# Query features turned by transposing DMAs instead of TensorE, and a table of offsets on the scheduler's priorities

## The chip, the cores and the metric

The kernel runs on one core of a Trainium2 chip. The metric is the device time of one execution in microseconds (us); lower is better. The core's engines are called as the profile calls them: PE (TensorE matmuls) and PEld (its weight loads), DVE (VectorE), ACT (ScalarE), POOL (GpSimd) and SP (SyncE, which in this kernel issues every DMA). Each engine works through its own queue in order and waits on semaphores.

## The reference

Two attention layers over 2048 tokens, 1024 columns and 32 heads of 32 columns are computed from separate inputs, and their outputs stand side by side. All data are float32.

```python
# A: four segments of 512 tokens; softmax attention inside a segment, a linear memory between them
logits = einsum("bhqd,bhkd->bhqk", qs, ks) * scale + mask
a_dot  = einsum("bhqk,bhkd->bhqd", softmax(logits), vs)
a_mem  = einsum("bhld,bhde->bhle", phi(qs), M) / (einsum("bhld,bhd->bhl", phi(qs), z)[..., None] + 1e-6)
o = g * a_mem + (1.0 - g) * a_dot          # then o @ wo
# B: linear attention with learned features
pq, pk = q @ w_phi, k @ w_phi              # per head
phi_q = concat([softmax(pq), softmax(-pq)]);  phi_k = concat([softmax(pk), softmax(-pk)])
kv, z = einsum("bhsf,bhsd->bhfd", phi_k, v), einsum("bhsf->bhf", phi_k)
o = einsum("bhqf,bhfd->bhqd", phi_q, kv) / (einsum("bhqf,bhf->bhq", phi_q, z)[..., None] + 1e-6)   # then o @ wo
```

The change lies in B's query side: a head has 64 features (32 of each softmax), a token 2048 in all.

## The kernel before, in words

Float32 accuracy is had from float16 matmuls: every operand is split into a high half (a rounded copy, made on ACT) and a low half (the rest, made by a subtraction on DVE or POOL), and each product is three matmuls: high by high, high by low, low by high. Products with large weights are done in seven block products of 512 columns by Strassen's scheme (`strassen`, L572 for loads of its operand and L584 for its matmuls) or block by block (`product`, L370).

The program has these stages in time: A's projections and attention together with the preparation of B's weights and inputs (to about 870 us); B's values and key features, which end in `kls`, the key-value sums of 32 heads split into halves (to about 1260 us, L1445); B's query features and output (1240 to 1565 us); A's output projection (L1636, from 1565 us to the end). The stages overlap at their seams.

In the query stage the 2048 tokens are 16 chunks of 128. For every pair of chunks, `strassen` makes four results of 128 tokens by 512 columns. `expo` turns each into `e`, 128 tokens by 1024 float32 features, with maxima, minima, two subtractions (L1238 to L1242, DVE), four exponentials (ACT) and sums (L1248, DVE). For each chunk and each half `hb` of the heads (32 times in all) there follow:

- POOL multiplies `e` by the key sums (L1550) and DVE reduces to denominators `dn` (L1553 to L1561); POOL multiplies `e` by the result (L1563).
- PE turns `e` so that features lie on partitions: eight float32 transposes of 128 by 128 into PSUM (L1569), in two groups of four. ACT copies each group of four, scaled by 2**14, to float16 (L1571), and DVE makes the low half from the same PSUM bank (L1573). The two halves are `pt`.
- PE multiplies `pt` by `kls` in 24 small matmuls (L1582, tile `pv`), and ACT and DVE split the result into `ot` (L1586, L1588).

When both halves of a chunk's `ot` are there, `project` multiplies them by B's output weight: twice 24 matmuls of 128 by 512 into a `misc` bank (L370), a scaled copy by ACT (L1463) and a store issued by SP (L1465).

The order of all instructions on each engine is not the order of the code. `Graph.op` records every operation with an engine, an estimated duration, what it reads and writes, and a priority `prio`; `Graph.run` then walks a clock, and at each step, for the engine that can start first, emits the operation with the smallest priority among those that could start then. Priorities are numbers per unit of work: in the query stage a chunk c has `P = Q0 + c`, `strassen` has `P - 1.2`, the features `P` and `project` `P + 1.1`. Estimated durations, DMA transfer times included, so decide the order, and the hardware then follows that order with its own durations. Tiles come from pools with a fixed number of buffers: `e` has five, `pt` three, `ot` four.

## Time and profile before

| | us |
|---|---|
| median of 3 runs | 1734.23 (1733.72 to 1735.37) |
| the profiled execution's own time | 1733.96 |
| its span, first to last instruction | 1732.3 |
| PE busy in the span | 1697.2 |
| DVE busy | 1384.0 |
| ACT busy | 1157.8 |
| POOL busy | 939.5 |

Busy time is the time in which at least one instruction of an engine was in work. Matmuls overlap each other in the pipeline, so what a matmul costs is read from the distance between the starts of successive ones and not from its duration: in a run of 128 by 512 matmuls the starts are 0.216 us apart, where the duration of one is given as 0.38 us. The profile's idle times of an engine are put down to what ended them.

### The profile page before, as it was taken

The page shows a single profiled execution, that of the slowest core. Times are in us where ns is not written, and L with a number is a line of the kernel's source. Part 1 is how long each engine was busy: PE and PEld are TensorE (multiplying, and loading weights), DVE is VectorE, ACT ScalarE, POOL GpSimd, SP SyncE. Part 2 cuts the span into 40 slices and gives each one's busy share as a digit, 9 for nine tenths or more (in the row PEclk, how much of TensorE's full clock was granted, in tenths as well). Part 3 has the DMA queues.
Part 4 walks back from the last instruction along what each step waited for, and adds up shares of the span by engine and source line. Part 5 has one row for each costly group of instructions (what it writes and reads, how often), then busy time and mean ns, then how long its engine had stood idle before and what let it go on. Part 6 is the DMA issues. An engine that isn't in the chain of part 4 may idle for free.

```text
span 1732.3 us, 39104 instructions
## 1 busy us (share of the span) xinstructions
PE 1697.2 (98%) x14664; PEld 1030.3 (59%) x14664; DVE 1384.0 (80%) x3269; ACT 1157.8 (67%) x2131; POOL 939.5 (54%) x1184
## 2 busy tenths in 40 slices
PE   8999999999999999999999999999999999999999
PEld 6667666767776676776754444444545555554444
DVE  6889899999997787889874988877978877786541
ACT  8788889888888798677772676765545544444331
POOL 3346477754478866656651777645737675440000
PEclk9999999999999999999999999999999999999999
DMA  6556455775666664743467474567413332234311
GB/s 210 160 166 185 151 169 174 223 209 169 224 181 185 188 165 122 227 162 106 136 179 262 131 240 130 180 211 251 161 44 118 103 111 85 63 139 146 122 66 63
DMA packets 194141, 273.62 MB, mean 158 GB/s; under 512 B 72224, under 2 KB 125216, under 8 KB 187424
## 3 DMA queue, kind: packets, MB, share of 16 engines
q1 hardware_dynamic: 193952, 271.13, 49.5%
q8 instruction: 115, 1.88, 0.4%
q14 instruction: 74, 0.61, 0.1%
HBM read 160.12 MB, written 85.00 MB: 142 GB/s over the span
## 4 chain that ended last, share of the span: by engine, by line
PE 40%; DVE 11%; ACT 2%; POOL 1%; issue 1%; POOLq 0%; ACTq 0%; DVEq 0%
PE proj L584 14%; PE misc L370 7%; PE proj L1636 5%; PE s L1636 2%; PE proj L370 2%; PE s L584 2%; DVE mx L1238 2%; PE misc L1636 1%; DVE r L1248 1%; PE pv L1582 1%; PE misc L584 1%; PE s L1569 1%; DVE e L1240 1%; DVE dn L1553 1%; DVE e L1242 1%; DVE pt L1389 1%
## 5 line engine op out<-in xcount | busy, mean ns | idle before, releaser
L370 PE MATMUL proj<-S,S 128*128 128x128 f16 (+1 forms) x3072 | 507.1, 300 | 4.3 <-DVE S L405 1.9
L370 PEld LDWEIGHTS <-S 128*128 128x128 f16 x4608 | 328.7, 98 | 151.2 <-issue 10.8
L584 PE MATMUL proj<-S,S 128*128 128x512 f16 x1584 | 360.6, 379 | 2.4 <-ACT cs L590 2.4
L584 PEld LDWEIGHTS <-S 128*128 128x128 f16 x2016 | 192.7, 98 | 221.7 <-issue 3.3
L960 POOL TENSOR_SCALAR_AFFINE_SELECT ph<-ph 128x256 f16<-128x256 f16 (+1 forms) x448 | 191.6, 450 | 172.5 <-DVE ph L954 133.7
L852 DVE CUSTOM_DVE_ANT_0 s<-s,causal 128x512 f32<-128x512 f32 (+3 forms) x512 | 242.6, 510 | 10.3 <-PE s L846 7.0
L954 DVE SCALAR_TENSOR_TENSOR ph<-s,ph 128x512 f16<-128x512 f32 x320 | 209.6, 683 | 51.5 <-ACT ph L953 49.3
L953 ACT ACTIVATE ph<-s 128x512 f16<-128x512 f32 x320 | 190.2, 659 | 0.3
L370 PE MATMUL misc<-S,ot 128*128 128x512 f16 x768 | 174.9, 380 | 0.0
L1245 ACT ACTIVATE e<-e,sk 128x256 f32<-128x256 f32 x256 | 113.4, 498 | 65.5 <-DVE e L1242 60.8
L370 PEld LDWEIGHTS <-ot 128*128 128x128 f16 x768 | 73.4, 98 | 81.8 <-issue 0.9
L846 PE MATMUL s<-S 96*128 96x512 f16 (+3 forms) x512 | 113.9, 299 | 2.2 <-DVE ph L954 1.6
L947 PE MATMUL s<-S 104*128 104x512 f16 (+3 forms) x512 | 113.1, 299 | 2.2 <-DVE ph L954 1.5
L951 ACT ACTIVATE s<-s,os 128x512 f32<-128x512 f32 x160 | 106.2, 717 | 6.9 <-PE s L947 5.3
L1550 POOL TENSOR_TENSOR e<-e,zb 128x512 f32<-128x512 f32 x64 | 80.2, 1277 | 55.7 <-DVE r L1248 35.1
L951 ACT ACTIVATE s<-s,bd 128x512 f32<-128x512 f32 x160 | 105.4, 705 | 6.5 <-PE s L947 6.4
L370 PE MATMUL proj<-wv,S 128*128 128x128 f16 x1536 | 101.8, 219 | 0.0
L983 PEld LDWEIGHTS <-ph 128*128 128x128 f16 x2560 | 87.3, 96 | 18.1 <-issue 2.2
L983 PE MATMUL pv<-vl,ph 128*128 128x66 f16 (+1 forms) x2560 | 91.9, 184 | 2.0 <-DVE oall L987 1.0
L1248 DVE TENSOR_REDUCE r<-e 128x32 f32<-128x1024 f32 x64 | 77.1, 1206 | 16.2 <-ACT e L1245 16.2
L1563 POOL TENSOR_TENSOR e<-e,r 128x1024 f32<-128x1024 f32 x32 | 61.9, 1938 | 34.5 <-DVE r L1561 27.5
L852 DVE DVE_READ_ACCUMULATOR2_ANT mt<- 128x1 f32 x512 | 72.6, 142 | 0.0
(344 smaller groups left out, 3344.1 us busy)
## 6 DMA issues: line engine op xcount, KB each, us to landing
S<-xf_d SPq DMA_DIRECT2D x126, 256.0 KB
S<-h SPq DMA_DIRECT2D x192, 128.0 KB
S<-wf_d SPq DMA_DIRECT2D x21, 1024.0 KB
st<-bwqk SPq DMA_DIRECT2D x64, 256.0 KB
out<-os SPq DMA_DIRECT2D x40, 256.0 KB
S<-aw SPq DMA_DIRECT2D x16, 512.0 KB
wa_d<-S SPq DMA_DIRECT2D x16, 512.0 KB
wf_d<-fo SPq DMA_DIRECT2D x32, 256.0 KB
```

The source lines that it names most:

```text
L370: op(PE, dur, lambda c=c, a=a, b=b, lv=lv, rv=rv: nc.tensor.matmul(pv(), lv(), rv(), start=(c == 0 and a + b == 0), stop=(c == n - 1 and a ...
L584: op(PE, 0.215, lambda n=n, a=a, b=b, lv=lv, rv=rv: nc.tensor.matmul(ps(), lv(), rv(), start=(start and n == 0 and a + b == 0), stop=(n == ...
L846: nc.tensor.matmul(ps()[:, o:o + 128 * i + 128], st()[0:96, 0, h, 128 * i:128 * i + 128], st()[0:96, 1, h, 0:128 * i + 128], start=True, s ...
L852: dve(0.12 + 0.00113 * n, lambda h=h, i=i, o=o, n=n: nc.vector.tensor_tensor_reduce(ps()[:, o:o + n], ps()[:, o:o + n], causal[:, 512 - n: ...
L947: nc.tensor.matmul(ps()[:, o:o + n], st()[0:104, 1, h, 128 * j:128 * j + 128], st()[0:104, 0, h, 128 * j:512], start=True, stop=True)
L951: act(0.59, lambda: nc.scalar.activation(ps(), ps(), AF.Exp, bias=0.0, scale=bdv()[:, 3, i2, 0:1]), r=[(bd, i2)], w=[ps])
L953: act(0.5, lambda: nc.scalar.activation(ph()[:, 0], ps(), AF.Copy, scale=2.0 ** 14), r=[ps], w=[(ph, 0)])
L954: dve(0.6, lambda: nc.vector.scalar_tensor_tensor(ph()[:, 1], ps(), 2.0 ** 14, ph()[:, 0], op0=OP.mult, op1=OP.subtract), r=[ps, (ph, 0)], ...
L960: nc.gpsimd.affine_select(pd, pd, pattern=[[0, n], [1, 128]], compare_op=OP.is_ge, fill=0.0, base=0, channel_multiplier=-1)
L983: nc.tensor.matmul(ps()[:, i, n0:n1], ph()[:, a, o:o + 128], vl()[:, j, h, n0:n1], start=(i == 0 and a == 0), stop=(j == min(i, 2)), skip_ ...
L1245: op(ACT, 0.41, lambda i=i: nc.scalar.activation(e()[:, 4 * i:4 * i + 4], e()[:, 4 * i:4 * i + 4], AF.Exp, bias=0.0, scale=sk()[:, i:i + 1 ...
L1636: op(PE, 0.215, lambda n=n, a=a, b=b: nc.tensor.matmul(ps(), v(a)[:, n, :], wform[w]()[:, b, n, :], start=(start and n == 0 and a + b == 0 ...
```

## The change

The change has two parts.

First, the query features are turned by DMA. After POOL's last multiplication, ACT makes the float16 high half directly from `e` in SBUF (two instructions of 128 by 512), DVE subtracts it from `e` to get the low half (two instructions, now `tensor_tensor` between SBUF tiles), and both halves go into a new tile `eh`, which is taken from the same five buffers as `e`. One DMA then transposes all sixteen 128 by 128 float16 blocks of `eh` into `pt`, 512 KB per DMA. The eight PE transposes and the PSUM banks they used are gone. The factor 2**14, which ACT and DVE applied, is now folded into the small row `r` before POOL's multiplication. The planner is told 0.6 us of SP and about 4.2 us to landing for such a DMA.

Second, `Graph.op` numbers the stretches of consecutive recorded operations that have the same priority ("jobs") and adds an offset from the table `MOVES`, by engine and job, to the priority of each operation in it. The table has 238 entries, from -43 to +21.5, spread over jobs 20 to 363; jobs are recorded in the order of the code, from A's first unit to the last chunks of the query stage. Since priorities alone choose between operations that are ready, the table changes the order on all five queues through most of the program.

```diff
+MOVES = {
+    "PE": {
+        20: -6.5, 22: -12.5, 76: -7, 79: -15.5, 83: -4, 96: -5, 101: 2, 102: 4, 104: 2, 107: 5.5, 108: 15.5, 113: 1.5,
...
     def op(self, eng, dur, fn, r=(), w=(), prio=0, lat=0.0, short=False, port=False, need=(), kb=256):
+        if prio != self.job[0]:
+            self.job = prio, self.job[1] + 1
+        prio += MOVES.get(eng, {}).get(self.job[1], 0.0)
...
+    def ev(e):
+        return e().rearrange("p h s d -> p (h s d)")
+
...
-            op(DVE, 0.1, lambda d1=d1, r=r: nc.vector.tensor_tensor(
-                r(), r(), d1()[:, :, None].to_broadcast([128, 16, 2]), op=OP.mult), r=[d1, r], w=[r], prio=P)
+            op(DVE, 0.1, lambda d1=d1, r=r: nc.vector.scalar_tensor_tensor(
+                r(), r(), 2.0 ** 14, d1()[:, :, None].to_broadcast([128, 16, 2]), op0=OP.mult, op1=OP.mult), r=[d1, r], w=[r], prio=P)
...
             pt = G.buf("b", [128, 2, 8, 128], F16, "pt", 3)
+            eh = G.buf("b", [128, 16, 2, 32], F32, "e", 5)
+
+            def hv(eh=eh):
+                return eh().rearrange("p h s d -> p (h s d)").bitcast(F16).rearrange("p (a n) -> p a n", a=2)
+
             for q in range(2):
-                ps = bank("s", [128, 4, 128])
-                for i in range(4):
-                    op(PE, 0.11, lambda q=q, i=i, e=e, ps=ps: nc.tensor.transpose(
-                        ps()[:, i, :], pairs(e)[:, 4 * q + i, :], ident), r=[e], w=[ps], prio=P)
-                op(ACT, 0.55, lambda q=q, pt=pt, ps=ps: nc.scalar.activation(pt()[:, 0, 4 * q:4 * q + 4], ps(), AF.Copy, scale=2.0 ** 14),
-                   r=[ps], w=[(pt, (0, q))], prio=P)
-                op(DVE, 0.62, lambda q=q, pt=pt, ps=ps: nc.vector.scalar_tensor_tensor(
-                    pt()[:, 1, 4 * q:4 * q + 4], ps(), 2.0 ** 14, pt()[:, 0, 4 * q:4 * q + 4], op0=OP.mult, op1=OP.subtract),
-                   r=[ps, (pt, (0, q))], w=[(pt, (1, q))], prio=P)
+                op(ACT, 0.53, lambda q=q, e=e, hv=hv: nc.scalar.activation(
+                    hv()[:, 0, 512 * q:512 * q + 512], ev(e)[:, 512 * q:512 * q + 512], AF.Copy), r=[e], w=[(eh, (0, q))], prio=P)
+                op(DVE, 0.7, lambda q=q, e=e, hv=hv: nc.vector.tensor_tensor(
+                    hv()[:, 1, 512 * q:512 * q + 512], ev(e)[:, 512 * q:512 * q + 512], hv()[:, 0, 512 * q:512 * q + 512], op=OP.subtract),
+                   r=[e, (eh, (0, q))], w=[(eh, (1, q))], prio=P, port=True)
+            op(SP, 0.6, lambda pt=pt, hv=hv: nc.sync.dma_start_transpose(
+                pt().rearrange("p a g t -> p (a g) t"), hv().rearrange("p a n -> p (a n)")),
+               r=[(eh, (a, q)) for a in range(2) for q in range(2)], w=[pt], prio=P, lat=2.0, kb=512)
```

What the orders of instructions become is shown at three places, each before and after. Names are those of the tiles; line numbers of the kernel after are 26 to 33 higher than those of the kernel before for the same statement.

PE in the query stage, at the end of a `strassen` (tile `proj`). Before, twelve transposes of `e` into an `s` bank stand here, and then a chunk's `project` (tile `misc`, from `ot`):

```order
L584 LDWEIGHTS S_14955
L584 MATMUL proj<-S_19188,S_14955 128x512
L1569 MATMUL s<-ident,e 128x128 x12
L370 LDWEIGHTS ot
L370 MATMUL misc<-S_19610,ot 128x512
```

After, at the end of a `strassen` of the same stage:

```order
L610 LDWEIGHTS S_15057
L610 MATMUL proj<-S_19210,S_15057 128x512
L1615 LDWEIGHTS kls
L1615 MATMUL pv<-pt,kls 64x128
L1615 LDWEIGHTS kls
```

The transposes are gone, and the products of `pt` and `kls` follow directly; they now wait for a DMA.

SP in the query stage. Before, a chunk's stores of the output (`out<-os`) stand together, then the loads of the next operand of `strassen` (`xf_d`):

```order
L1511 DMA wo_d<-cs 256x1x512
L1480 DMA h_20449<-awo 128x1024
L1465 DMA out<-os 128x512 x3
L572 DMA S_13978<-xf_d 128x1024 x4
L572 DMA S_14955<-xf_d 128x1024
```

After, transposing DMAs and stores of the output take turns:

```order
L1494 DMA out<-os 128x512
L1606 DMA_TRANSPOSE pt<-e 128x16x128
L1494 DMA out<-os 128x512
L1606 DMA_TRANSPOSE pt<-e 128x16x128
L1494 DMA out<-os 128x512
L1540 DMA wo_d<-cs 256x1x512
```

A store in this queue waits until ACT has copied the `project` result, and a transposing DMA behind it waits as long.

DVE at the seam between the key features and the query stage, around the last subtraction that makes `kls` (of the half of the heads that comes second). Before:

```order
L1440 TENSOR_TENSOR ez<-ez,zs 128x512
L1240 TENSOR_TENSOR e<-cs,mx 128x16x32
L1242 TENSOR_TENSOR e<-mx,cs 128x16x32
L1238 TENSOR_REDUCE mx<-proj 128x16
L1573 SCALAR_TENSOR_TENSOR pt<-s,pt 128x512 x2
L1238 TENSOR_REDUCE mx<-proj 128x16
L1242 TENSOR_TENSOR e<-mx,proj 128x16x32
L1445 TENSOR_TENSOR kls<-ez,kls 128x512
L1573 SCALAR_TENSOR_TENSOR pt<-s,pt 128x512 x2
```

After:

```order
L620 TENSOR_TENSOR proj<-cs,proj 128x512
L1589 RECIPROCAL d_19679<-d_19679 128x16
L1585 TENSOR_TENSOR dn<-dn,r 128x32
L1264 TENSOR_REDUCE mx<-cs 128x16
L1590 SCALAR_TENSOR_TENSOR r<-r,d_19679 128x32
L1587 SCALAR_TENSOR_TENSOR d_19690<-dn 128x16
L1474 TENSOR_TENSOR kls<-ez,kls 128x512
L1603 TENSOR_TENSOR e<-e 128x512 x2
```

Before, this last row of `kls` stands behind six of the subtractions that split query features (L1573; two of the six are shown). After, it stands ahead of all of them (L1603).

More of the change, by code (lines that the diff above doesn't have):

```diff
@@ L56 @@
 EUP = 2.0 ** 15
+MOVES = {
[6 rows of a table added]
+    "DVE": {
[4 rows of a table added]
+    "ACT": {
[3 rows of a table added]
+    "POOL": {
+        59: 0.5, 67: 5.5, 70: -0.5, 93: -6, 141: 5, 154: -8, 173: 3, 199: 12, 202: -3, 211: -16.5, 234: -5.5, 238: -29.5,
+        250: -2, 252: 1.5, 257: 0.5, 312: -11.5, 326: -7},
+    "SP": {
+        88: 5, 89: 2.5, 107: -2.5, 131: 3, 134: 21.5, 183: 8, 184: -7, 223: 6.5, 226: -9, 238: -37},
+}
 def view(t, off, ap):
@@ L92, in __init__ @@
         self.ops, self.tags, self.pools, self.opened, self.lines = [], {}, pools, {}, {}
+        self.job = (None, -1)
     def buf(self, pool, shape, dtype, tag, bufs=1):
```

11 rows, old and new, of the table MOVES are left out of this document.

## The prediction

> **What bounds the kernel now.** I read the busy times first, then busy time by stage, then what PE waits for, and last the chain of work that ended last inside the query stage. The page's head and its busy line:
>
> ```profile
> span 1732.3 us, 39104 instructions
> PE 1697.2 (98%) x14664; PEld 1030.3 (59%) x14664; DVE 1384.0 (80%) x3269; ACT 1157.8 (67%) x2131; POOL 939.5 (54%) x1184
> ```
>
> PE is idle for 35.1 us in all. The view by stages (start:end, length, then busy us of PE, PEld, DVE, ACT, POOL, the granted clock, DMA share, GB/s) says where:
>
> ```profile
> 0.00:80.00 80.00, 71.18 (x557) 49.57 (x558) 58.82 (x170) 63.61 (x108) 28.79 (x61) 0.94 0.58 187
> 80.00:1240.00 1160.00, 1144.33 (x11135) 739.88 (x11134) 989.94 (x2527) 885.91 (x1645) 726.07 (x988) 1.00 0.59 183
> 1240.00:1280.00 40.00, 34.57 (x269) 19.34 (x267) 38.07 (x66) 17.65 (x36) 25.85 (x20) 0.96 0.11 34
> 1280.00:1565.00 285.00, 283.92 (x1948) 147.54 (x1945) 226.68 (x406) 133.95 (x257) 158.78 (x116) 1.00 0.32 104
> 1565.00:1733.00 168.00, 163.18 (x773) 73.98 (x767) 70.53 (x104) 56.70 (x86) 0.00 (x0) 1.00 0.25 92
> ```
>
> PE idles 8.8 us at the start, 15.7 us over 1160 us of attention and key features, 5.4 us in the 40 us where the query stage begins, 1.1 us in the rest of that stage and 4.8 us in the last stage. So from 1280 us on only PE's own work sets the time, and what leaves PE there shortens the run one for one. In the 40 us before that DVE is the full engine (38.07 of 40 us), and the longest single wait of PE is on it (columns of the first rows: total us, times, longest; no other wait of PE is longer than the 1.7 of the second row):
>
> ```profile
> PE pv L1582 <- DVE kls L1445: 4.0, 1, 4.0
> PE misc L381 <- ACT S L445: 3.2, 2, 1.7
> 1260.10 0.68 DVE L1445 TENSOR_TENSOR kls<-ez,kls 128x512 f16<-128x512 f32 x1
> 1260.84 3.16 PE L1582 MATMUL pv<-pt,kls 128*64 128x128 f16 x68 [3.99 <-DVE kls L1445]
> ```
>
> The chain in the steady part of the query stage runs on PE alone, which gives the price of its pieces (start, length, engine, tile, line, count):
>
> ```profile
> 1392.10 1.31 PE s L1569 x12
> 1393.41 1.29 PE misc L370 x6
> 1394.71 0.44 PE s L1569 x4
> 1395.14 1.51 PE misc L370 x7
> ```
>
> Twelve transposes hold PE for 1.31 us, 0.109 us each; a matmul of 512 columns for 0.216 us.
>
> **The PE transposes leave.** The rows of the pieces that go, and of the nearest to those that come (L1389 and L1386 make the same split, from `e` in SBUF, for the key features):
>
> ```profile
> L1569 PE MATMUL s<-ident,e 128*128 128x128 f32 x256 | 33.6, 274 | 1.1 <-POOL e L1563 1.1
> L1571 ACT ACTIVATE pt<-s 128x512 f16<-128x512 f32 x64 | 34.6, 592 | 29.4 <-PE s L1569 29.4
> L1573 DVE SCALAR_TENSOR_TENSOR pt<-s,pt 128x512 f16<-128x512 f32 x64 | 41.0, 680 | 3.0 <-ACT pt L1571 2.8
> L1386 ACT ACTIVATE pt<-e 128x512 f16<-128x512 f32 x64 | 37.5, 620 | 27.6 <-PE kv L1396 14.3 <-POOL e L1354 12.9 <-POOL pt L1389 0.4
> L1389 DVE TENSOR_TENSOR pt<-e,pt 128x512 f16<-128x512 f32 x32 | 29.9, 948 | 4.5 <-ACT pt L1386 4.4
> ```
>
> PE loses 256 transposes. By their duration that would be more, but they are pipelined: 256 x 0.109 = 27.9 us of the path. The first pair's 32 (3.5 us) lie where DVE is full, so they are not given back: +3.5 us against it.
>
> **The split moves to SBUF.** ACT's 64 pieces go from 0.592 to about 0.620 us, +1.8 us on an engine busy for 134 of 285 us: nothing. DVE's 64 go from 41.0 us in all to between 41 (same price) and 64 x 0.948 = 60.7 us (the mean of L1389, which stretches where POOL holds the port they share), 0 to +19.7 us. DVE has 58.3 us idle from 1280 to 1565 us, and PE's shorter work takes some 25 of them. So 33 us remain to cover 19.7: I take 0. If that cover goes, PE waits in turn; that is a rival below. The small row `r` (L1561) becomes another form of the same 128 by 32 elements: 0. POOL's work is unchanged. 64 allocations of an `s` bank are gone: 0, since PE's waits in this stage sum to 1.1 us.
>
> **32 transposing DMAs come.** The trace has none, so I bound the time T from issue to landing. From below: a plain load of the same 512 KB, alone in the queue. SP issues it at 1590.55; in the view of DMA over 1589 to 1599 us (40 slices of 0.25 us, busy tenths) its run of digits ends at about 1593.5:
>
> ```profile
> 1590.55 0.33 SPq L1601 DMA_DIRECT2D e<-oa_d  x1
> DMA  0000798000948899700000000200000000079800
> q1 hardware_dynamic: 193952, 271.13, 49.5%
> ```
>
> So T is not under 3.0 us. From above: the block rows are 128 float16, 256 bytes, which makes 2048 runs of a 512 KB tile; at the mean packet of the whole run (0.495 x 16 engines x 1732.3 us / 193952 = 0.0707 us, of 1398 bytes) 2048 / 16 x 0.0707 = 9.05 us, and with the 0.95 us between issue and first slice T = 10.0 us. I take 5 us, nearer the plain load, since that moves the same bytes.
>
> What waits for it: SP issues one behind a store of `out` (the rows of SP's order), so the DMA starts after the `project` half ahead of it on PE, ACT's copy and the issue:
>
> ```profile
> L1463 ACT ACTIVATE os<-misc,wo 128x512 f32<-128x512 f32 x32 | 21.9, 684 | 27.9 <-PE misc L370 21.5 <-issue 2.9 <-DMA out<-os 2.1
> ```
>
> Counting the matmuls on PE between that half and the `pv` that reads the DMA's `pt` (0.216 us for 512 columns), the shortest stretch is 9.2 us and the median about 13 us. Off go 0.4 us to ACT's start, 0.68 us for the copy and 0.33 us for the issue: 7.8 us of cover at the least, 11.6 us at the median. T = 5 costs nothing; T = 10 costs the shortfalls of eight stretches, 8.9 us. Range of this term: 0 to +9, taken 0. Each DMA also takes some 0.3 to 0.7 us of SP, which mostly waits. The 32 x 512 KB raise the DMA share of 0.32 by 32 x 2.1 / 285 = 0.24 (by 1.0 at 9 us, which would delay the operand loads). `eh` doubles the tiles taken from the five buffers of `e` and holds its buffer until the DMA lands, so the next pair's subtractions (L1240) can wait on it; in the five buffers a pair of about 42 us has 210 us of place, so 0 at T = 5.
>
> At this place a page speaks against the change. The Trainium skill, "VectorE: DVE Perf Modes", section "The three transpose paths", gives 1309 ns for one 128 by 128 block by DMA against 390 ns on TensorE; the trace has 274 ns for TensorE's and none for the DMA's. Its page "Advanced Engine Details and Errata", section "X-Bar Transpose (TRN2)", says instead that transposing DMAs are as fast as regular ones, which is the lower bound above. By the first, if blocks went one after another, T would be an estimated 20.9 us.
>
> **The table of offsets.** It moves work on all queues. At the one place where PE waits long the order says what happens: `kls` is made ahead of all query splits, so its 4.0 us go. Elsewhere PE has 15.7 us of idle time in 1160 us, in waits of at most 2 us; a new order can take them all away or as well double them: -15.7 to +15.7, taken 0.
>
> **The sum**, against the profiled execution's own 1733.96 us (0.3 us under the median of the runs): 1733.96 - 27.9 + 3.5 - 4.0 = 1705.6, so 1706 us.
>
> **Rivals.**
>
> (a) DVE becomes the bound of the query stage. From 1240 to 1565 us it is busy for 264.8 us; with 19.7 more it has 284.4 us of work in a stage that shrinks from 325 to about 297, 96%. At 95%, at the seam, PE idled 5.4 of 40 us; against it stands that with 79% of DVE PE idled only 1.1 of 285. At the seam's rate over 297 us PE would lose 40 us, half of that is as likely: 1706 + 20 = 1726 us, still faster. The price of the split (over 0.85 us in the mean) decides.
>
> (b) The other side: the sixteen blocks of a transposing DMA go one after another, and `pt` is late every time. Place: `pv` (L1582) on PE. Against it stands that 512 KB plain took 3.0 us; for it, that this trace shows nothing of how a transpose moves. With cover of 11.6 us at the median and eight pairs whose four DMAs overlap fully or not at all, each us of T above 11.6 costs 8 to 32 us. The gain of 28.4 us is eaten at T of 12.5 to 15.2 us, and at T = 20.9 the time is 1706 + 9.3 x (8 to 32), 1780 to 2003 us. The page on the three paths would have it so.
>
> (c) The gain of the table is larger: half of the 15.7 us goes too, 1698 us.
>
> (d) The change does less than it says, because the freed PE time reappears as waits on ACT and DVE all along: within 0.2%, 1734 us.
>
> **Chances.** The forecast (with c inside its own range of 1690 to 1718 us) 0.60; (a) 0.18, of which 0.02 ends slower; (b) 0.13; (d) 0.05; 0.04 is left for an order that loses more than 28 us in the 1160 us before. The range of 1688 to 1745 us takes in the forecast, (a) and (d), and leaves out (b) beyond its beginning and the best of (c). A difference within 0.2%, 3.5 us, is about what a measurement of this kernel can't tell from none. Faster: 0.60 + 0.16 + 0.02 of (b) at its beginning = 0.78; same 0.05; slower 0.17.
>
> **What would show it.** No rows of L1569 and 256 fewer PE instructions; busy PE down by some 33 us in durations, and the query stage shorter by 24 to 30 us; no wait of `pv` on `kls`; waits of `pv` on the DMA of `pt` under 10 us in all; DVE's new split at 0.68 to 0.95 us. Wrong: `pv` waiting for `pt` by several us each time, SP stuck at L1606, DVE busy at 95% with PE idle beside it, or the attention stage longer than now by more than its 15.7 us of idle.

## The result, and the profile after

The changed kernel takes 1724.18 us in the median of four runs (1721.16 to 1726.32), the kernel before, beside it, 1733.97 (1732.22 to 1735.37). The ratio is 0.9943, 95% interval 0.9923 to 0.9962: faster by some 10 us, where the forecast had 28.

The head and the busy line of the page of the kernel after (its profiled execution took 1722.68 us):

```profile
span 1721.0 us, 38652 instructions
PE 1670.3 (97%) x14408; PEld 1002.9 (58%) x14408; DVE 1408.9 (82%) x3269; ACT 1159.6 (67%) x2131; POOL 955.2 (56%) x1184
```

PE lost 26.9 us of busy time (1697.2 to 1670.3) and gained 15.6 us of idle time (35.1 to 50.7 us); the difference is the 11.3 us by which the span is shorter. Where the idle time stands is seen in the view by stages, first of the kernel before, then of the kernel after (start:end, length, busy us of PE, PEld, DVE, ACT, POOL, granted clock, DMA share, GB/s):

```profile
0.00:1200.00 1200.00, 1176.93 (x11421) 768.03 (x11422) 1010.89 (x2617) 927.31 (x1708) 731.40 (x1029) 1.00 0.59 182
1200.00:1280.00 80.00, 73.14 (x536) 40.75 (x534) 75.93 (x145) 39.86 (x81) 49.30 (x39) 0.98 0.37 129
1280.00:1565.00 285.00, 283.92 (x1948) 147.54 (x1945) 226.68 (x406) 133.95 (x257) 158.78 (x116) 1.00 0.32 104
```

```profile
0.00:1200.00 1200.00, 1183.90 (x11462) 772.90 (x11463) 1005.71 (x2631) 933.68 (x1718) 738.81 (x1036) 1.00 0.59 183
1200.00:1280.00 80.00, 64.50 (x451) 33.31 (x450) 75.66 (x136) 37.24 (x73) 44.36 (x33) 0.89 0.48 141
1280.00:1565.00 285.00, 270.00 (x1796) 128.02 (x1795) 258.23 (x401) 135.11 (x260) 172.01 (x117) 0.99 0.61 155
```

Up to 1200 us PE idles 16.1 us where it idled 23.1: 7.0 us won. No DMA of the change lies there, so this is a matter of order, and most of it is the table's: with the table alone PE idles 17.5 us there, with the DMAs alone 21.7. In the 80 us of the seam it idles 15.5 us where it idled 6.9: 8.6 us lost. In the next 285 us, where PE had been idle for 1.1 us, it idles 15.0: 13.9 us lost. The last stage is as before. So 26.9 + 7.0 - 8.6 - 13.9 = 11.4 us. DVE's busy time beside it went from 226.7 to 258.2 of 285 us, and POOL's over the whole span from 939.5 to 955.2 us.

What PE waits for (total us, times, longest), the three largest of the kernel after:

```profile
PE pv L1615 <- DMA pt<-e: 21.3, 8, 11.0
PE proj L610 <- ACT cs L616: 6.1, 4, 3.1
PE proj L610 <- DVE cs L620: 2.2, 2, 1.6
```

The wait of `pv` on `kls` is gone; that on the transposing DMA of `pt` has come, half of it in one place. A wait is put down to what came last, and the DMA was itself started late. Its chain at the seam, from the timelines of ACT, DVE, SP and PE of the kernel after (start, length, instruction, idle before it):

```profile
1232.17 1.15 ACT L1601 ACTIVATE e<-e 128x512 f16<-128x512 f32 x2 [6.45 <-POOL e L1592]
1238.96 0.68 DVE L1474 TENSOR_TENSOR kls<-ez,kls 128x512 f16<-128x512 f32 x1
1239.57 3.00 DVE L1603 TENSOR_TENSOR e<-e 128x512 f16<-128x512 f32 x2
1242.63 9.03 SPq L1606 DMA_TRANSPOSE pt<-e  x3
1247.06 1.49 PE L1615 MATMUL pv<-pt,kls 128*64 128x128 f16 x24 [11.04 <-DMA pt<-e]
1251.61 5.28 PE L610 MATMUL proj<-S,S 128*128 128x512 f16 x12 [3.06 <-ACT cs L616]
```

The view by stages for the last of these rows (columns as above; the granted clock is the third from the end):

```profile
1251.00:1257.00 6.00, 5.39 (x16) 1.76 (x17) 5.78 (x10) 2.31 (x7) 2.74 (x2) 0.50 1.08 211
```

The high half is there at 1233.3 us, but DVE, full, does what its order has first until 1239.6; two subtractions take 3.0 us, and from SP's issue to `pv` pass 4.4 us. The idle 11 us have a cost behind them: twelve matmuls, 2.6 us at the 0.216 us of the kernel before, take 5.28 us at a granted clock of 0.50.

The subtraction of the split, in the view of groups of DVE of the kernel after (busy us, mean ns of one):

```profile
L1603 DVE TENSOR_TENSOR e<-e 128x512 f16<-128x512 f32 x64 | 75.9, 1221 | 12.4 <-ACT e L1601 12.2
L1268 DVE TENSOR_TENSOR e<-mx,proj 128x512 f32<-128x512 f32 x34 | 22.9, 673 | 2.5 <-DMA pt<-e 2.4
L1268 DVE TENSOR_TENSOR e<-mx,cs 128x512 f32<-128x512 f32 x16 | 16.1, 1009 | 0.1
```

Its 64 pieces take 75.9 us where they took 41.0, and the forecast's upper bound was 60.7. The second and third row are one statement with its source in PSUM (`proj`) and in SBUF (`cs`): 673 and 1009 ns. Of the two, only the one with both sources in SBUF is stretched.

### The profile page after: what moved, and what is told of

It is laid out like the page before. It is cut to its first block, busy times and chain, and to the rows that moved or that the text cites. A ratio compares the mean times of both kernels' runs of the same rounds, so it can differ in the third digit from the quotient of the medians.

```text
span 1721.0 us, 38652 instructions
## 1 busy us (share of the span) xinstructions
PE 1670.3 (97%) x14408; PEld 1002.9 (58%) x14408; DVE 1408.9 (82%) x3269; ACT 1159.6 (67%) x2131; POOL 955.2 (56%) x1184
## 4 chain that ended last, share of the span: by engine, by line
PE 45%; DVE 15%; DMA 2%; ACT 2%; issue 1%; POOL 1%; SPq 0%; DVEq 0%; ACTq 0%; POOLq 0%
PE proj L610 14%; PE proj L396 8%; PE proj L1669 5%; PE s L610 3%; PE misc L396 3%; DVE e L1603 3%; PE s L1669 2%; DMA pt<-e 2%; PE misc L610 2%; DVE mx L1264 2%; DVE r L1274 1%; DVE dn L1582 1%; PE pv L1009 1%; PE s L973 1%; PE misc L1669 1%
## 5 line engine op out<-in xcount | busy, mean ns | idle before, releaser
L610 PE MATMUL proj<-S,S 128*128 128x512 f16 x1584 | 368.4, 381 | 8.3 <-ACT cs L616 6.1
L878 DVE CUSTOM_DVE_ANT_0 s<-s,causal 128x256 f32<-128x256 f32 (+3 forms) x512 | 242.9, 508 | 14.1 <-PE s L872 10.8
L1579 POOL TENSOR_TENSOR e<-e,zb 128x512 f32<-128x512 f32 x64 | 86.1, 1369 | 56.5 <-DVE r L1274 45.4
L1601 ACT ACTIVATE e<-e 128x512 f16<-128x512 f32 x64 | 37.3, 622 | 97.0 <-POOL e L1592 47.5
L1274 DVE TENSOR_REDUCE r<-e 128x32 f32<-128x1024 f32 x64 | 76.6, 1207 | 12.5 <-ACT e L1271 12.4
```

Source lines behind the costliest of these rows:

```text
L610: op(PE, 0.215, lambda n=n, a=a, b=b, lv=lv, rv=rv: nc.tensor.matmul(ps(), lv(), rv(), start=(start and n == 0 and a + b == 0), stop=(n == ...
L878: dve(0.12 + 0.00113 * n, lambda h=h, i=i, o=o, n=n: nc.vector.tensor_tensor_reduce(ps()[:, o:o + n], ps()[:, o:o + n], causal[:, 512 - n: ...
```

## The experiments

Ratios are to the kernel before, run beside it on the same chip, with 95% intervals. The expectations call 947 ns the mean of a piece of L1603; that is the median, and the mean is 1221 ns. "Theory DVE" says that the subtractions hold PE up, "theory DMA" that the transposing DMA does.

**The table alone.** The kernel before with the table (it has 166 entries, not 238).

```diff
+MOVES = {
...
+        if prio != self.job[0]:
+            self.job = prio, self.job[1] + 1
+        prio += MOVES.get(eng, {}).get(self.job[1], 0.0)
```

> The table of offsets alone: the query features are still transposed on PE, only the order is the changed kernel's. After stood at 1213.3 us where before stood at 1225.8 us at the last key-feature transposes, so if the table made the gain, this kernel already takes about 10 us less than before (1720 to 1727 us) and the transposing DMAs add nothing. If the DMAs made the gain and the table only shifts where PE waits, it stays within 3 us of 1734.

1722.2 us (1721.88 to 1726.88), ratio 0.9948 [0.9935, 0.996]. The table alone gains as much as the whole change.

**The DMAs alone.** The kernel after with an empty table.

```diff
-MOVES = {
...
+MOVES = {}
```

> The transposing DMAs alone, with an empty table. Theory DVE (the split from SBUF at 947 ns keeps DVE at 37 to 39 of 40 us and PE waits in turn): 1730 to 1738 us, nothing left of the 28 us of transposes that PE lost. Theory DMA (a transposing DMA lands too late for its pv): the same time, but with the long waits of pv on the DMA of pt spread over all pairs. If instead the table's early key rows cost the seam its 11 us, this kernel is the faster one: 1710 to 1718 us.

1723.41 us (1721.98 to 1727.34), ratio 0.9953 [0.9939, 0.9967]: the DMAs alone gain it too, some 8 us, so no branch of the expectation held. The two gains don't add up. PE's idle time (length less busy, same view) shows why: in the three stretches it is 17.5, 4.5 and 1.9 us with the table alone, 21.7, 12.5 and 11.0 with the DMAs alone, 16.1, 15.5 and 15.0 with both. The DMAs alone give back as idle time 14.3 us of the 26.3 us of PE's work that they save. With the table PE comes to the seam earlier, but the first `pv` starts at 1247.1 us against 1249.9 with the DMAs alone and 1243.3 in the kernel before: the lead is spent waiting there.

**No DMA.** The split is written into `pt`.

```diff
-            eh = G.buf("b", [128, 16, 2, 32], F32, "e", 5)
...
-            op(SP, 0.6, lambda pt=pt, hv=hv: nc.sync.dma_start_transpose(
...
+            def hv(pt=pt):
+                return pt().rearrange("p a g t -> p a (g t)")
...
```

> The changed kernel without the 32 transposing DMAs: ACT and DVE write the split straight into pt, so the features reach pv untransposed (this part of the computation is left out), and the buffers that held the split for the DMA are free. DVE does the same work at the same places. Theory DVE: within 4 us of the changed kernel (1719 to 1727 us), PE's waits go from the DMA to DVE. Theory DMA: the 4.4 us from issue to pv and the 2.2 us on SP go, PE's 21.3 us of waits on the DMA with them: 1702 to 1710 us.

1717.12 us, ratio 0.9914 [0.9899, 0.9928], 5 us below the kernel after by the ratios. PE waits all the same, now under DVE's name:

```profile
PE pv L1610 <- DVE pt L1601: 16.2, 10, 4.1
```

The time lies between the two ranges, nearer theory DVE's; but the order isn't that of the kernel after, since the planner follows the code.

**Half of the subtractions on POOL.**

```diff
+                sub, ns, d = (POOL, nc.gpsimd, 1.28) if q else (DVE, nc.vector, 0.7)
-                op(DVE, 0.7, lambda q=q, e=e, hv=hv: nc.vector.tensor_tensor(
+                op(sub, d, lambda q=q, e=e, hv=hv, ns=ns: ns.tensor_tensor(
```

> The changed kernel with half of the split's subtractions (32 of 64) on POOL instead of DVE. Theory DVE: DVE loses 30 us of the 37 to 39 of 40 us that it is busy for in the query stage, and the kernel gains 5 to 15 us (1709 to 1719 us), if POOL's piece of about 2 us isn't late itself. Theory DMA: the features come later by about 1 us a half and the time is the same or up to 6 us longer (1724 to 1730 us).

1706.13 us (1704.81 to 1707.15), ratio 0.9847 [0.9834, 0.9861]: 16 to 18 us less than the kernel after, beyond theory DVE's range. PE's idle time from 1280 to 1565 us falls from 15.0 to 2.5 us; at the seam it stays at 15.0.

**The same without the table.**

```diff
-MOVES = {
...
+MOVES = {}
```

> The transposing DMAs with half of the split's subtractions on POOL and an empty table: with the run before it, which had the table, this prices the table where DVE isn't full. If the table's lead of 12.5 us at the last key-feature transposes lasts, this kernel is about 9 us slower than that run (1713 to 1717 us). If the lead is spent waiting for the first pair's features, which are made by a full DVE at the same time in both (first pv at 1246.1 us with the table, 1249.9 us in the run with the DMAs alone), 3 to 4 us are left of it: 1709 to 1711 us.

1726.62 us, ratio 0.9971 [0.9956, 0.9985]. Both branches miss it: here the table is worth 21 us. PE idles 21.4, 13.2 and 14.1 us, so 11.6 of the 21 us lie in the query stage. With an empty table `pv` waits there although DVE has less to do, and the time is no shorter than with the DMAs alone (1723.41): in that order, taking work off DVE gained nothing.

**The subtraction in another form.**

```diff
-                op(DVE, 0.7, lambda q=q, e=e, hv=hv: nc.vector.tensor_tensor(
+                op(DVE, 0.7, lambda q=q, e=e, hv=hv: nc.vector.scalar_tensor_tensor(
...
```

> The changed kernel with the subtraction of the split in the form that the kernel before used on a PSUM source (SCALAR_TENSOR_TENSOR, times one, both sources still in SBUF). If the 947 ns in the mean come from the form TENSOR_TENSOR, which stood at 948 ns in the key features too, the pieces go to about 680 ns, DVE loses 17 us and the kernel takes 1710 to 1718 us. If they come from having both sources in SBUF beside a busy POOL, nothing moves: 920 to 970 ns and 1720 to 1726 us.

1721.24 us, ratio 0.9941 [0.9921, 0.9962], the second branch: the row doesn't move, so it isn't the form.

```profile
L1603 DVE SCALAR_TENSOR_TENSOR e<-e 128x512 f16<-128x512 f32 x64 | 76.0, 1222 | 12.3 <-ACT e L1601 12.2
```

**Half on POOL, the first pair of blocks on PE.** A block of queries is a chunk of 128 tokens here.

```diff
+            if c < 2:
+                for q in range(2):
+                    ps = bank("s", [128, 4, 128])
...
```

> Half of the subtractions on POOL, as in the run at 1706.1 us, and the first pair of blocks transposed on PE as before the change, DMAs from the second pair on. That run's only large wait is the 10.5 us at the first pv. If it is the chain of split, issue and landing of the first transposing DMA that PE waits for, the wait falls to about 3 us for 32 transposes of 3.5 us more: 1699 to 1704 us. If it is DVE's order ahead of the split, PE waits as long for the split from PSUM: 1705 to 1711 us.

1715.64 us, ratio 0.9905 [0.9889, 0.9922], slower than without the edit. The seam did as the first branch had it (the wait at the first `pv` is 2.7 us, PE idle 4.5 of 80 us), but PE idles 16.4 us from 1280 to 1565, 7.3 of them in one wait at 1379 us: the changed code got another order, with the offsets laid out for the old one. One experiment changed two things here.

**Each DMA cut in two.**

```diff
...
+                op(SP, 0.6, lambda q=q, pt=pt, hv=hv: nc.sync.dma_start_transpose(
+                    pt()[:, q].rearrange("p a g t -> p (a g) t"), hv()[:, q].rearrange("p a n -> p (a n)")),
+                   r=[(eh, (a, q)) for a in range(2)], w=[(pt, q)], prio=P, lat=2.0, kb=256)
...
```

> The changed kernel with each transposing DMA of 512 KB cut into two of 256 KB, the first issued as soon as its half of the split is done. If the time from issue to landing goes with the size, the second half has about 2.2 us left to do when the last subtraction ends, pv waits some 2 us less each time and the kernel takes 1714 to 1721 us. If it has a large fixed part, 64 issues of some 2 us keep SP from the operand loads and it takes 1723 to 1735 us.

1712.19 us, ratio 0.9883 [0.9863, 0.9903]: below the range given, some 10 us less than the kernel after. SP's rows, first of the kernel after (512 KB), then of this one (256 KB; ns, least, median, most):

```profile
L1606 SPq DMA_TRANSPOSE pt<-e x32: 1322/2164/4082, 1242.6 to 1551.9; - x32
```

```profile
L1606 SPq DMA_TRANSPOSE pt<-e x64: 1231/1262/2560, 1241.5 to 1540.6; - x64
```

So both theories seemed to have a share, but most of the experiments so far mixed the cost with a new order. The next two leave every engine's order as in the kernel after, since they tell the planner the same costs, and take away one cost each.

**No subtraction, same order.**

```diff
-                op(DVE, 0.7, lambda q=q, e=e, hv=hv: nc.vector.tensor_tensor(
-                    hv()[:, 1, 512 * q:512 * q + 512], ev(e)[:, 512 * q:512 * q + 512], hv()[:, 0, 512 * q:512 * q + 512], op=OP.subtract),
+                op(DVE, 0.7, lambda q=q, e=e, hv=hv: nc.vector.memset(
+                    hv()[:, 1, 512 * q:512 * q + 512], 0.0),
```

> The changed kernel in exactly its order on every engine, but each of the 64 subtractions of the split on DVE (947 ns in the mean) is replaced by filling the low half with zeros; the planner still counts 0.70 us for each. The low half of the query features is left out of the result. The order's own schedule, in the planner's costs, ends at 1699 us, and the chip takes 1721. If the 22 us are lost because the subtractions take longer than planned for and pv comes late behind them, the kernel takes 1701 to 1710 us. If the DMA loses them, it stays at 1718 to 1724 us.

1699.28 us, ratio 0.9803 [0.978, 0.9826], beyond the first branch: 0.9943 - 0.9803 is 24 us of 1733, give or take 5 by the two intervals. The DMAs are all there, and after the seam they cost nothing; the row that took 75.9 us, and the stretch from 1280 us:

```profile
L1603 DVE MEMSET e<- 128x256 uint32 x64 | 17.4, 272 | 3.7 <-DMA pt<-e 3.5
...
1280.00:1565.00 285.00, 284.79 (x1876) 134.93 (x1875) 221.15 (x420) 145.78 (x273) 153.48 (x114) 1.00 0.63 163
```

58.5 us less on DVE make the kernel 24 us shorter. In this order, then, the subtractions cost more than the whole 18 us by which the result missed the forecast, as theory DVE has it. The fill replaces the whole subtraction, not only its stretch; the stretch alone is priced by the run with the other source in PSUM. POOL's busy time is back at 938.7 us here.

**Half of each DMA, same order.**

```diff
-                pt().rearrange("p a g t -> p (a g) t"), hv().rearrange("p a n -> p (a n)")),
+                pt()[:, 0], hv()[:, 0]),
...
-                        nc.tensor.matmul(pn()[64 * k:64 * k + 64, g, :], kls()[:, a, 8 * hb + 2 * g + k, :], pt()[:, b, 2 * g + k, :],
+                        nc.tensor.matmul(pn()[64 * k:64 * k + 64, g, :], kls()[:, a, 8 * hb + 2 * g + k, :], pt()[:, 0, 2 * g + k, :],
```

> The changed kernel in exactly its order, split and all, but each transposing DMA moves only the high half (256 KB in place of 512) and pv reads that in place of the low half too, so the low half of the query features is left out of the result. If the DMA's time from issue to landing loses the 22 us, it takes 1703 to 1712 us. If the subtractions on DVE lose them, it stays near 1716 to 1724 us.

1714.58 us, ratio 0.9891 [0.9869, 0.9912]: 9 us less than the kernel after, in between. With DVE late, a shorter DMA gives back part of the lateness; PE now waits for `cs` instead (the subtractions still take 76.4 us of DVE):

```profile
PE proj L610 <- ACT cs L616: 21.4, 6, 14.1
```

**Halved DMAs and half on POOL together.**

```diff
+                sub, ns, d = (POOL, nc.gpsimd, 1.28) if q else (DVE, nc.vector, 0.7)
...
+                op(SP, 0.6, lambda q=q, pt=pt, hv=hv: nc.sync.dma_start_transpose(
+                    pt()[:, q].rearrange("p a g t -> p (a g) t"), hv()[:, q].rearrange("p a n -> p (a n)")),
```

> Half of the subtractions on POOL (1706.1 us alone) and each transposing DMA cut into two halves (1712.2 us alone). The planner's schedule ends at 1699 us for this one and for both of those. If the two take away different losses, 1698 to 1703 us; if they only shorten the same chain ahead of pv, 1703 to 1708 us.

1711.37 us, ratio 0.9874 [0.9852, 0.9895]: slower than with POOL alone, outside both branches. It isn't shown why (see the last experiment but one).

**Truer costs for the planner.**

```diff
-                op(DVE, 0.7, lambda q=q, e=e, hv=hv: nc.vector.tensor_tensor(
+                op(DVE, 0.95, lambda q=q, e=e, hv=hv: nc.vector.tensor_tensor(
...
-            op(SP, 0.6, lambda pt=pt, hv=hv: nc.sync.dma_start_transpose(
+            op(SP, 2.2, lambda pt=pt, hv=hv: nc.sync.dma_start_transpose(
```

> The changed kernel with truer costs for the planner: 0.95 us for a subtraction of the split in place of 0.70, and 2.2 us of SP for a transposing DMA in place of 0.6. The work is the same, only the order follows. By those costs the planner's schedule with this table ends at 1724 us in place of 1699. If the chip takes what the schedule says plus a few us, as it did for the kernels with half of the subtractions on POOL, it is 1725 to 1730 us, slower than the changed kernel although the costs are truer. If truer costs let PE wait less, 1705 to 1718 us.

1731.46 us, ratio 0.9989 [0.9978, 1.0], as slow as the kernel before: the first branch, and 1.5 us past its range. Telling the planner truer numbers didn't help here: the order that it makes with the same offsets is longer by its own count too (1723.8 us in the table below).

The walk of `Graph.run` ends at a time of its own, the sum of the planner's costs along its order. It is no time of the chip, but it says what an order would give if every cost were as planned. Beside the spans of the profiled executions (us):

```
kernel                          planner   chip   difference
before                           1729.2  1732.3    3.1
table alone                      1715.0  1725.2   10.2
DMAs alone                       1715.3  1720.3    5.0
no DMA                           1691.9  1715.6   23.7
after                            1699.1  1721.0   21.9
after, no subtraction            1699.1  1697.4   -1.7
after, half of each DMA          1699.1  1712.4   13.3
after, one source                1699.1  1709.5   10.4
half on POOL                     1699.8  1705.0    5.2
half on POOL, no table           1723.6  1724.9    1.3
half on POOL, first pair on PE   1713.0  1714.3    1.3
truer costs                      1723.8  1728.6    4.8
DMAs in halves                   1699.8  1709.7    9.9
halves, half on POOL             1699.3  1710.1   10.8
source in PSUM                   1697.7  1705.0    7.3
source in PSUM, halves           1698.5  1709.8   11.3
source in PSUM, first block PE   1696.9  1700.5    3.6
```

The kernel after and the one without the DMA fall furthest behind their own orders, 21.9 and 23.7 us; without the subtractions the chip keeps to the order of the kernel after. So the lag is there without the DMAs and gone without the subtractions. It is a lag in this order: in the kernel with the DMAs alone a subtraction takes 1124 ns in the mean, nearly as long, and that kernel falls back by 5.0 us only, in an order that was 16 us longer by plan. (The row with one source and the last three belong to runs told below.) Two misses on kernels with half on POOL, without the table and with the first pair on PE, are in the first column: their orders were worse already. The third, with halves, is not: it falls 10.8 us behind.

**One source, same order.** The subtraction replaced by a multiplication of `e` by a constant.

```diff
...
+                op(DVE, 0.7, lambda q=q, e=e, hv=hv: nc.vector.tensor_scalar(
+                    hv()[:, 1, 512 * q:512 * q + 512], ev(e)[:, 512 * q:512 * q + 512], 2.0 ** -12, None, op0=OP.mult),
```

> The changed kernel in exactly its order, the subtraction replaced by a DVE operation on the same 128 by 512 elements with one source (a fixed multiple of e is written as the low half, so the true low half of the query features is left out of the result). If the second source in SBUF beside a busy POOL makes the 1221 ns that a piece takes in the mean, this one takes 700 ns or less and the kernel 1699 to 1704 us, as with the subtraction left out. If any operation of this size there costs the time, it takes 1710 us or more.

1710.9 us, ratio 0.9866 [0.985, 0.9883], the time of the second branch, but not as meant: the piece itself is still stretched with one source. So it doesn't take a second source: this operation takes 410 ns at the least, 946 in the median and 1005 in the mean.

```profile
L1603 DVE TENSOR_SCALAR e<-e x64: 410/946/2139, 1239.8 to 1537.0; 128x512 f16<-128x512 f32 x64
```

So 61.9 us on DVE cost some 11 us more (by the ratios) than the 17.4 of the fill, and 13 less than the 75.9 of the subtraction. Not every read from SBUF is stretched, though: the sums over `e` (L1582), 64 `TENSOR_REDUCE` of 128 by 512 from SBUF, take 665 ns in the mean in the kernel after. The Trainium skill, "SBUF — State Buffer", section "SBUF: two separate sides", says that DVE and GpSimd exclude each other on a shared port for a whole instruction, when DVE's operation has two sources in SBUF or runs in a mode that uses two ports. The rows agree with it: 410 ns alone is faster than the 620 to 690 ns of the others, so that piece runs in another mode, and it is stretched like the subtraction, while the sums are not. That it is another mode is an inference from its time alone.

What each piece waited for can be read piece by piece, from DVE's timeline beside POOL's. Three rows of the kernel after:

```profile
1289.15 1.71 POOL L501 TENSOR_TENSOR h<-h,h 128x512 f32<-128x512 f32 x1
1289.66 1.75 DVE L1603 TENSOR_TENSOR e<-e 128x512 f16<-128x512 f32 x1
1291.94 0.67 DVE L1603 TENSOR_TENSOR e<-e 128x512 f16<-128x512 f32 x1
```

The first subtraction begins while a POOL instruction is in work and ends at 1291.41 us, 0.55 us after that one's end; the second begins beside none and takes 0.67 us. So it is with nearly all 64: the 27 that begin with no POOL instruction in work take 674 to 693 ns, and of the 37 that begin beside one, 35 end 545 to 551 ns after its end. With one source 28 pieces begin beside none and take 410 to 428 ns, and 34 of the other 36 end 281 to 287 ns after POOL's instruction. A piece, then, pays what is left of POOL's instruction. POOL waits in turn: its busy time is 15.7 us longer than before the change, and as before without the subtractions.

**The other source in PSUM.** ACT copies each half of `e` into a PSUM bank, and DVE subtracts from that.

```diff
...
+                ps = bank("s", [128, 512])
+                op(ACT, 0.53, lambda q=q, e=e, ps=ps: nc.scalar.activation(ps(), ev(e)[:, 512 * q:512 * q + 512], AF.Copy), r=[e], w=[ps], prio=P)
+                op(DVE, 0.62, lambda q=q, ps=ps, hv=hv: nc.vector.tensor_tensor(
+                    hv()[:, 1, 512 * q:512 * q + 512], ps(), hv()[:, 0, 512 * q:512 * q + 512], op=OP.subtract),
```

> The changed kernel with one more copy of each half of the features on ACT (64 of some 0.6 us) into a PSUM bank, and DVE's subtraction reading that copy and the high half in SBUF, as before the change it read PSUM and pt. Nothing of the computation is left out. If both sources in SBUF make the stretch, the 64 pieces go from 1221 to about 680 ns (75.9 to 43 us) and the kernel takes 1700 to 1706 us. If the stretch is not from the sources, or ACT's 38 us more come late, it takes 1712 us or more.

1707.11 us (1706.18 to 1708.15), ratio 0.985 [0.9835, 0.9865], 1 us above the first branch, with the subtraction at its old price and ACT's 37.4 us more hidden. The 33 pieces that begin beside a POOL instruction take 627 to 692 ns, as the others do, and POOL's busy time is 939.0 us. The order is another one here, but by plan only 1.4 us shorter. The subtraction, the new copy, the stretch from 1280 us and the one long wait that is left:

```profile
L1605 DVE TENSOR_TENSOR e<-s,e 128x512 f16<-128x512 f32 x64 | 42.7, 679 | 11.3 <-ACT s L1604 10.7 <-POOL h L501 0.4
...
L1604 ACT ACTIVATE s<-e 128x512 f32<-128x512 f32 x64 | 37.4, 586 | 1.3 <-POOL e L1592 1.3
...
1280.00:1565.00 285.00, 283.52 (x1870) 134.25 (x1869) 236.35 (x421) 170.08 (x323) 155.62 (x115) 1.00 0.63 164
...
PE pv L1617 <- DMA pt<-e: 10.4, 1, 10.4
```

**The same with each DMA cut in two.**

```diff
...
+                op(SP, 0.6, lambda q=q, pt=pt, hv=hv: nc.sync.dma_start_transpose(
+                    pt()[:, q].rearrange("p a g t -> p (a g) t"), hv()[:, q].rearrange("p a n -> p (a n)")),
```

> As the run before, and each transposing DMA cut into two of 256 KB. If the DMA's length is hidden once DVE is in time, within 3 us of the run before; if it is still on the path, 4 to 10 us less.

1712.73 us, ratio 0.9881 [0.9866, 0.9895]: 5 us slower, where it was expected equal or faster. All three kernels with halved DMAs span 1709.7 to 1710.1 us, whether the subtraction costs 1094 ns (on DVE), is shared with POOL or costs 682 ns. Something that comes with 64 issues or with their order limits them; no run here tells which.

**The first block on PE.** As the run with PSUM, the first 16 transposes on PE.

```diff
+            if c == 0:
+                for q in range(2):
+                    ps = bank("s", [128, 4, 128])
...
```

> As the run with the second source in PSUM (1707.1 us), but the first block of queries is transposed on PE, 16 transposes of 1.7 us in all, and the DMAs begin with the second block. If the first DMA, some 4.4 us from issue to pv, holds the 10.4 us at the first pv, the waits of PE up to 1280 us fall by 4 us or more and the kernel takes 1702 to 1705 us. If DVE's work ahead of it holds it, PE waits as long in another place: 1705 to 1710 us.

1702.46 us (1701.37 to 1705.02), ratio 0.9828 [0.9811, 0.9844], the fastest kernel here that computes everything: some 30 us less than before and 20 less than after, and the first branch. PE is busy for 71.3 us of the seam's 80 where it was 63.8, and what is left there are waits on DVE:

```profile
1200.00:1280.00 80.00, 71.33 (x520) 37.86 (x520) 79.27 (x147) 43.20 (x84) 47.75 (x37) 0.94 0.48 143
...
PE pv L1629 <- DVE kls L1474: 3.0, 1, 3.0
PE pv L1629 <- DVE pt L1603: 2.9, 2, 2.5
```

At the seam, then, the first DMA's 4.4 us are on the path, as theory DMA had it for that place; behind it, with the subtraction in time, they aren't.

## Why the prediction was right or wrong

**PE's transposes, -27.9 us: right.** PE's busy time fell by 26.9 us, and the kernel without the subtraction, at 1699 us, shows that all of it can reach the end.

**The split on DVE, "0 to +19.7", taken at 0: this step failed, twice.** The size was outside its bounds: 75.9 us where 41.0 stood, +34.9. The row taken for the upper bound (L1389, 948 ns) is from another stage, where POOL makes the other 32 of the 64 subtractions and 15 of DVE's 32 begin beside a POOL instruction; in the split of the kernel after it is 37 of 64. Two rows of the query stage itself, with both sources in SBUF, stood at 1095 and 932 ns in the kernel before, the first of them beyond the bound too:

```profile
L1242 DVE TENSOR_TENSOR e<-mx,cs 128x512 f32<-128x512 f32 x7 | 7.7, 1095 | 0.0
L1240 DVE TENSOR_TENSOR e<-cs,mx 128x512 f32<-128x512 f32 x7 | 6.5, 932 | 0.0
```

And the cover was wrong: the step set DVE's idle time over 285 us, 58.3 us, against the new work. That is an average. Each subtraction stands in a chain, POOL's product, ACT, two subtractions, SP, DMA, `pv`, whose place on PE was fixed by a planner that counted 0.70 us for it and let it begin only between POOL's instructions (`port=True`); DVE still had 26.8 us idle in the 285 us, and PE idled for 15.0. And "POOL's work is unchanged" left out that POOL waits as well, +15.7 us of busy time. What was measured in place of 0: with the subtraction at its old price the chip takes 1707 us, so the stretch costs some 16 us by the ratios, in an order that is nearly the same by plan; without any subtraction, in the same order, the chip takes 24 us less, give or take 5. The 8 us between the two are the old price and the copy on ACT that the run with PSUM adds; no run parts them. Put into the sum with the table's 7.0 us, 1705.6 + 24 - 7.0 = 1722.6, beside 1722.7 for the profiled execution. That it meets to 0.1 us is luck, since the sum still holds the forecast's -0.5 for the seam, which came out otherwise.

**Rival (a) was the nearest.** "DVE becomes the bound" gave 1726 us, with a split over 0.85 us in the mean as the point that decides; it came out at 1.22 and 1724. Its condition was met, and it had the wait in the right place, but its 20 us were half of a rate taken from the seam, so that the time came within 2 us is in part luck. DVE was no bound either: it reached 91% of 285 us (258.2), not 95%, and its lateness in the chain did the harm. Every row with both sources in SBUF that was looked at stood above 0.85 us already (932 to 1095 ns, the prediction's own L1389 at 948 among them), so 0.18 was low for what was on record.

**The transposing DMA, T = 5 us, cost 0: T right, cost right under a condition.** From issue to `pv` it took 4.4 us at the seam, and in the steady part as well:

```profile
1361.18 1.72 SPq L1606 DMA_TRANSPOSE pt<-e  x1
...
1365.54 0.86 PE L1615 MATMUL pv<-pt,kls 128*64 128x128 f16 x24 [3.27 <-DMA pt<-e]
```

Where the subtraction is in time, `pv` waits for it only at the seam, so the 7.8 us of cover held; where it is late, the DMA's length is part of the lateness, and halving it gave 9 us. SP's share was under-sized: 2.16 us in the median for an issue against "0.3 to 0.7". The DMA share rose from 0.32 to 0.61, somewhat more than the 0.24 reckoned from 2.1 us a DMA, a figure given without its working.

**Rival (b), blocks one after another: no.** The Trainium skill, "VectorE: DVE Perf Modes", section "The three transpose paths", gave 1309 ns a block, an estimated 20.9 us for sixteen; 4.4 us passed in all, so the trace doesn't agree for blocks that go in one DMA.

**The seam, +3.5 - 4.0: wrong.** The wait on `kls` did go, but PE waited 11.0 us near the same place, for the first split, which DVE, busy all of the 20 us up to 1240, begins at 1239.6 us, and then for its DMA. PE's idle time there rose by 8.6 us. It isn't the early `kls` that does it: with the DMAs alone `kls` is made behind the first split, and `pv` waits 8.7 us there. Nor is it the stretch alone: without the subtraction `pv` still waits 9.0 us.

**The table, taken at 0 within 15.7: a gain of some 6 to 7 us** of PE's idle time ahead of 1200 us (5.6 with the table alone, 7.0 in the kernel after), inside the bounds and about the 7.9 us of rival (c), whose 1698 us had no room for the subtraction.

**The signs.** Right: no transposes on PE and 256 fewer of its instructions, no wait on `kls`, no longer attention stage. Wrong: PE's busy time fell by 26.9 us, not by some 33; `pv` waits 21.3 us on the DMA instead of under 10; a piece of the split takes 1.22 us instead of 0.68 to 0.95; from the first `pv` to the last pass 312.6 us (1247.1 to 1559.7) where 322.0 passed (1243.3 to 1565.3), 9.4 less instead of 24 to 30.

## What to carry to other kernels

Moving a DVE operation's source from PSUM to SBUF changes its price where POOL is busy; look for a row of the same stage with its sources in the same place, take the mean, not the median, and ask how often a piece would begin beside a POOL instruction and how long that instruction is. Idle time of an engine summed over a stage is no cover for work that stands in a chain with a fixed place on another engine; ask what the order assumed for each link, and take one link away in the same order to price it. A table of offsets belongs to the code and the costs it was laid out for: an edit of what the planner sees gave another order here, and the same code with half on POOL took 1706 us with the table and 1727 without.

## What the runs showed of the hardware that was not expected

- A DVE subtraction of 128 by 512 with both sources in SBUF that began while a POOL instruction was in work ended 0.55 us after that instruction, in 35 of 37 cases, and took 674 to 693 ns with none beside it; a multiplication from one source in SBUF ended 0.28 us after it, and took 410 to 428 ns with none. A reduction from SBUF took 665 ns in the mean, and a subtraction with one source in PSUM 679 ns in the mean and 692 at the most, whether POOL was in work or not.
- One DMA transposed 512 KB of float16, sixteen blocks of 128 by 128, in 4.4 us from SP's issue to the first matmul that reads it; the issue held SP for 1.3 to 4.1 us, for 256 KB mostly for 1.26.
- After 11.0 us without work, 24 small matmuls and 3.1 us more without work, PE ran twelve matmuls in 5.28 us instead of 2.6, at a granted clock of 0.50; so this idle gap of PE cost more than its length.
